# FNet plus MLP in one pass: a lighter warm-up, one block's layernorm and stores moved ahead of the prepared DFT weights, and one output moved ahead of a form

## The chip, the cores and the metric

The kernel runs on one core of a Trainium2 chip. Its time is the device time of one execution in microseconds (us). The core has TensorE (PE in the profile), VectorE (DVE), ScalarE (ACT), GpSimd (POOL) and SyncE (SP), each with an instruction stream of its own that runs in order; they wait for one another by semaphores. DMA transfers are issued from the queues of SP, ACT and POOL.

## What is computed

For x of 2048 tokens by 640 features, all in f32:

```python
xn = _layernorm(x, axis=-1)
a = einsum("bsd,ed->bse", xn, dft_hid_re)      # DFT over the 640 features
b = einsum("bsd,ed->bse", xn, dft_hid_im)
y = einsum("ts,bse->bte", dft_seq_re, a) - einsum("ts,bse->bte", dft_seq_im, b)
h = gelu(einsum("bsd,df->bsf", xn, w1) + b1)    # 640 -> 1536
return x + y + (einsum("bsf,fd->bsd", h, w2) + b2)
```

## The kernel before

Every product of two f32 matrices is made of three matmuls: each operand is split into a high part that is rounded to fp32r and a low part that is the rest, and high·high, high·low and low·high are added in PSUM. `split` is the helper for it: ScalarE copies the high part (L160 in the profile), VectorE subtracts for the low part (L161). A product of 128 by 128 by 512 is therefore three lines L278, L279, L280, or a row of L304 in the hidden layer.

**Blocks.** The tokens are four blocks of 512 (16 chunks of 128). The front loads chunks 0 to 3, centers them (ScalarE chunk 1, VectorE chunks 0, 2 and 3), transposes them on TensorE into five PSUM banks, and splits each bank into XT. Ten matmuls on zeros (`warm_up`) stand ahead of the transposes on TensorE. The scale of the layernorm of block 0 is multiplied in later, ahead of the gelu.

**The main loop** runs g over 24 units: 12 groups of 128 hidden features for block 0, then 12 for block 1. In iteration g, TensorE makes `hidden(g+2)` (15 matmuls) and `output(g)` (15 matmuls), ScalarE makes `gelu(g+2)` and its high part hs, VectorE the low part of hs. Beside that, `second_block(i)` in the second half (g = 12 + i) prepares blocks 2 and 3, whose hidden layers are computed later by a scheme of seven products instead of eight (`head`, `mid`, `finish`, with the sums of x called forms a11, a12, a22, oa, ob, s1 to s4, and sums of w1 called tw).

**What lies around the change.** For a block, the normalized x goes to DRAM (`ln_apply`, 16 transfers to xs, L203) and comes back in another layout (`load_z`, L234). `prep_w(s)` turns pieces of the two 640 by 640 DFT matrices (wraw, turned to wt), forms sums of them and splits them into the tile wst, from which POOL's queue stores them to DRAM (wit, L418). A place in wst is written again by later calls, so the write waits until the store from it has landed. When the early calls of `prep_w` are over, `open_tw` gives wst's memory to other tiles, the first of them tw0, which `split_w1(0)` writes. `load_xo(1)` loads x once more for block 1, and `outs_at` adds block 1's outputs to it: VectorE turns a PSUM bank (L371) and POOL adds it (L373). `forms_ob` subtracts on VectorE, splits tw1 and the form ob.

All orders are written out by hand: the order of calls in the code is the order on each engine, and no scheduler changes it. Pools only decide which memory a tile lies in, and so which earlier transfer a write waits for.

Of the kernel before, what the change touches and what calls it, by code (L numbers as in the profile page):

```python
# [15 lines left out]
P = 128  # L16
Q = 4
B = 32
EPS = 1e-5
NWARM = 10  # L20
TAIL = 4
ASIDE = 1
PADL = 8
# [3 lines left out]
def kernel(  # L27
# [126 lines left out]
    def split(hi, lo, src, perm=False):  # L154

        h, l, s = (hi, lo, src)
        if perm:
            h, l = chunked(hi), chunked(lo)
            s = src.rearrange("p (q c i) -> p q c i", q=Q, i=B)
        nc.scalar.activation(h, s, AF.Copy)  # L160
        nc.vector.tensor_tensor(l, s, h.bitcast(F32), op=ALU.subtract)  # L161
# [125 lines left out]
    def unit(g):  # L287
        return g if g < NF else LATE[g % NF]

    def hidden(g, aside=None):  # L290
# [4 lines left out]
        if g == 0:  # L295
            steps = FIRST
        if g == 1:

            steps.sort(key=lambda s: s[1] == 2)
        for n, (j, k) in enumerate(steps):  # L300
            if aside and n == ASIDE:
                aside()
            a, b = kinds[k]
            nc.tensor.matmul(  # L304
                acc, W1[i][:, a, j * P : (j + 1) * P], XT[j][:, b], start=n == 0, stop=n == len(steps) - 1
            )
        return acc


    FIRST = [(0, 0), (0, 2), (1, 0), (1, 2), (0, 1), (2, 0), (2, 2), (1, 1), (3, 0), (3, 2)]  # L310
    FIRST += [(2, 1), (4, 0), (4, 2), (3, 1), (4, 1)]

    def gelu(g, acc, fill=lambda k: None):

# [347 lines left out]
            slots[key] = t[:, k * 2 * D : (k + 1) * 2 * D].rearrange("p (a b) -> p a b", a=2)  # L662
    nc.gpsimd.memset(eps, EPS)
    make_identity(nc, ident)
    nc.vector.memset(zeros, 0.0)
    warm = whole["as"][:, :TB]
    nc.vector.tensor_copy(warm, zeros)

    nc.scalar.activation(eps[:, 1:2], eps[:, 0:1], AF.Sqrt)
    load_w1(0, cuts=(0, 2, ND))  # L670
    load_w1(1, cuts=(0, 2, ND))

    wacc = bank(0)

    def warm_up():
        nc.tensor.matmul(wacc, warm[:, :P], warm, start=True, stop=True)

    for k in range(NWARM):
        warm_up()
    load_w1(2)  # L680
    load_w2(0)
    nc.sync.dma_start(b1c, b1.rearrange("(i p) -> p i", p=P))
    load_w2(1)
# [7 lines left out]
    def transpose_x(c, j0, j1):  # L691
        for j in range(j0, j1):
            nc.tensor.transpose(tacc[j][:, c * P : (c + 1) * P], xp[:, c, j * P : (j + 1) * P], ident)
# [10 lines left out]
    def center(c, op, shift, j0=0, j1=ND):  # L704
        nc.vector.tensor_scalar(
            chunked(xp[:, c])[:, :, j0:j1],
            xt[c].rearrange("p (q c i) -> p q c i", q=Q, i=B)[:, :, j0:j1],
            shift,
            None,
            op0=op,  # L710
        )
# [7 lines left out]
    ln_stats(0)  # L719
    center(0, ALU.subtract, MV[:, 0, 0:1])  # L720
    ln_stats(2)
    center(2, ALU.subtract, MV[:, 2, 0:1])
    sum_on_act(3)
    center(3, ALU.add, MV[:, 3, 5:6], 0, 2)
    center(3, ALU.add, MV[:, 3, 5:6], 2, ND)
    for lo, hi in ((0, 2 * P), (2 * P, D)):
        h, l = (W1[0][:, k, lo:hi] for k in range(2))
        nc.scalar.activation(h, first_w1[:, lo:hi], AF.Copy)
        nc.vector.tensor_tensor(l, first_w1[:, lo:hi], h.bitcast(F32), op=ALU.subtract)
    transpose_x(0, 0, ND)  # L730
    transpose_x(1, 0, ND)
    warm_up()
    for j0, j1 in ((0, 2), (2, ND)):
        transpose_x(2, j0, j1)
        transpose_x(3, j0, j1)
    for j in range(ND):
        split(XT[j][:, 0], XT[j][:, 1], tacc[j])
    load_w1(3)
    load_w1(4)
    for q in range(Q):  # L740
        nc.sync.dma_start(b2c[q * B : (q + 1) * B], b2[q * DQ : (q + 1) * DQ].rearrange("(c i) -> i c", i=B))
    acc0 = hidden(0)
    prep_w1(1)
    acc1 = hidden(1)

    nc.gpsimd.tensor_scalar(MV[:, 1::2, 0], MV[:, 1::2, 5], -1.0, None, op0=ALU.mult)
    square_on_act(1)
# [236 lines left out]
    def second_block(i):  # L984

        if i == 0:
            load_z(2)
            ln_stats(12)
            ln_stats(13)
        if i == 1:  # L990
            ln_stats(14)
            ln_stats(15)
        if i == 2:
            ln_scale(12, 4)
            for c in range(12, 16):
                ln_apply(c, nc.gpsimd if c < 14 else nc.sync)
        if i == 3:
            A["zs"] = place("xc01", (P, 30 * P), F32, name="zs")
            turn_z2(two(0), 0)
            turn_z2(two(2), 2)  # L1000
            turn_z1(ZT[:, 0], 4)
            load_z(3)
        if i == 4:
            form_of("a11", 0, two(0)[:, 0], lane("as", 5))
            open_xf()
        if i == 5:
            form_of("a11", 1, two(0)[:, 1], lane("xc23", 0))
            form_of("oa", 0, ZT[:, 0], lane("xc23", 1))
        if i == 6:
            form_of("a12", 0, two(2)[:, 0], lane("xc23", 2))  # L1010
            turn_z2(ZT, 2)
            turn_z2(two(4), 0)
            turn_z1(A["zs"][:, 6 * TB : 7 * TB], 4)
            load_xo(1)
            open_tw()
        if i == 7:
            sums_w1(0)
            split_w1(0)
            load_rq(1)
            form_of("a22", 0, ZT[:, 0], lane("r01", 0))  # L1020
        if i == 8:
            form_of("a22", 1, ZT[:, 1], lane("r01", 1))
            add(ZT, ZT, two(4))
        if i == 9:
            form_of("s1", 0, ZT[:, 0], lane("r01", 2))
            form_of("s1", 1, ZT[:, 1], lane("r01", 3))
            add(two(4), two(0), two(4), ALU.subtract)
            add(ZT, ZT, two(0), ALU.subtract)
# [18 lines left out]
        form_of("s4", 0, two(2)[:, 0], XTT[:, 3])  # L1047
        form_of("s4", 1, two(2)[:, 1], XTT[:, 4])

    w_early = {0: (0,), 1: (1,), 2: (2,), 3: (3,), 4: (4,), 5: (5,)}  # L1050
    prep_w1(3)
    gelu(1, acc1)
    for g in range(NG):
        t, i = divmod(g, NF)
        if t == 0:
            if i:
                prep_w1(i + 3)
            prep_w2(i + 1)
            load_w1(i + 6)
            load_w2(i + 4)  # L1060
            if i != 8:
                first_block(i)
            if i == NF - 1:
                open_w()
                acc = hidden(g + 2)
                output(g)

                def fill(k):
                    for e in ((0,), (1, 2))[k]:
                        add_block(xo[0], e, oacc[0][e], f"ot0_{e}", bias=b2c[:, e : e + 1])  # L1070

                gelu(g + 2, acc, fill)
                outs(0, (3, 4))
            elif i == NF - 2:
                output(g)
                gelu(g + 2, hidden(g + 2))
            else:
                acc = hidden(g + 2) if g else acc2
                if i == NF - 3:
                    for j in range(ND):  # L1080
                        prep_xt(1, j)
                        if j + 2 < ND:
                            transpose_z(1, j + 2)
                gelu(g + 2, acc)
                if i == 8:
                    first_block(i)
                if i == 9:
                    ln_stats(10)
                    ln_stats(11)
                output(g)  # L1090
        elif i < NF - 2:
            acc = hidden(g + 2)
            gelu(g + 2, acc)
            output(g)
            second_block(i)
            for k in w_early.get(i, ()):
                prep_w(k)
# [708 lines left out]
```

## Time and profile before

| | us |
|---|---|
| median of 3 runs | 850.71 (850.18 to 850.97) |
| the profiled execution | 853.42 |
| its span | 851.6 |
| PE busy | 842.5 (99%) |
| DVE busy | 668.0 (78%) |
| ACT busy | 355.3 (42%) |
| POOL busy | 53.6 (6%) |
| granted TensorE clock | 0.999 |

The span runs from the first to the last instruction of the profiled execution; 853.42 is the time of that same execution from outside. Matmuls overlap in the profile: one is shown as 0.39 us long although the next starts 0.23 us later, so starts are compared, not durations. In brackets behind a row stands how long its engine had been idle and who ended that.

### The profile page before, as it was taken

How to read it: one execution, taken by the hardware profiler on the slowest of the kernel's cores; microseconds unless marked ns; L12 is line 12 of the kernel's file. 1: busy time of each engine (PE TensorE's matmuls, PEld its weight loads, DVE VectorE, ACT ScalarE, POOL GpSimd, SP SyncE). 2: the span in 40 equal slices, each digit the busy share in tenths (PEclk: the TensorE clock that was granted, in tenths of full speed). 3: DMA queues.
4: the chain of work that ended last, by engine and by line, in shares of the span. 5: the costliest groups of instructions: out<-in, count | busy, mean ns of one | idle time of the engine just before them, and what ended most of it. 6: DMA issues, size and time to landing. Idle time of an engine off the chain costs nothing.

```text
span 851.6 us, 10345 instructions
## 1 busy us (share of the span) xinstructions
PE 842.5 (99%) x3707; PEld 694.5 (82%) x3707; DVE 668.0 (78%) x841; ACT 355.3 (42%) x499; POOL 53.6 (6%) x78
## 2 busy tenths in 40 slices
PE   8999999999999999999999999999999999999997
PEld 6888888778888888888888888888888888888886
DVE  6766764795757888879988787899977898885687
ACT  7454533555655554333434343232322423223241
POOL 0000313131221300000000000000000000000001
PEclk9999999999999999999999999999999999999999
DMA  6667799738669998948743669763865879805464
GB/s 185 187 185 186 162 215 252 196 79 195 207 216 347 360 218 158 188 102 204 164 137 95 177 211 285 171 139 97 213 164 171 253 184 228 312 18 179 124 170 108
DMA packets 207363, 158.45 MB, mean 186 GB/s; under 512 B 81040, under 2 KB 180880, under 8 KB 206800
## 3 DMA queue, kind: packets, MB, share of 16 engines
q1 hardware_dynamic: 198368, 134.59, 62.2%
q0 software_dynamic: 4400, 21.89, 6.5%
q10 hardware_dynamic: 4544, 1.31, 0.6%
q8 instruction: 29, 0.48, 0.2%
q14 instruction: 22, 0.18, 0.1%
HBM read 114.76 MB, written 42.99 MB: 185 GB/s over the span
## 4 chain that ended last, share of the span: by engine, by line
PE 83%; DVE 4%; DMA 4%; ACT 3%; issue 3%; SPq 2%; POOL 1%; ACTq 0%; POOLq 0%; DVEq 0%
PE banks L278 27%; PE banks L279 26%; PE banks L280 26%; PE banks L304 3%; DMA x<-in_A_x_dram 1%; DMA wit<-wst 1%; SPq L388 1%; DMA xs<-x 1%; ACT ab L322 1%; SPq L203 0%; SPq L178 0%; POOL wit L418 0%; DVE r L161 0%; ACT hs L326 0%; DVE tw L161 0%
## 5 line engine op out<-in xcount | busy, mean ns | idle before, releaser
L278 PE MATMUL banks<-as,xab 128*128 128x512 f32 x411 | 160.0, 389 | 0.6 <-DVE zs L371 0.6
L279 PE MATMUL banks<-as,xab 128*128 128x512 f32 x411 | 159.9, 389 | 0.0
L280 PE MATMUL banks<-as,xab 128*128 128x512 f32 x411 | 159.9, 389 | 0.0
L160 ACT ACTIVATE as<-r 128x1024 fp32r<-128x1024 f32 x80 | 85.0, 1062 | 177.9 <-PE banks L280 149.5
L161 DVE TENSOR_TENSOR as<-r,as 128x1024 fp32r<-128x1024 f32 x80 | 97.1, 1215 | 41.5 <-ACT as L160 41.5
L278 PEld LDWEIGHTS banks<-as,xab 128*128 128x128 f32 x411 | 77.2, 188 | 17.0 <-DVE zs L371 1.0
L279 PEld LDWEIGHTS banks<-as,xab 128*128 128x128 f32 x411 | 77.2, 188 | 16.0
L280 PEld LDWEIGHTS banks<-as,xab 128*128 128x128 f32 x411 | 77.2, 188 | 15.9
L278 PE MATMUL banks<-as,xc 128*128 128x512 f32 x224 | 87.1, 389 | 0.0
L279 PE MATMUL banks<-as,xc 128*128 128x512 f32 x224 | 87.1, 389 | 0.0
L280 PE MATMUL banks<-as,xc 128*128 128x512 f32 x224 | 87.1, 389 | 0.0
L160 ACT ACTIVATE as<-rt 128x1024 fp32r<-128x1024 f32 x32 | 34.0, 1063 | 70.5 <-PE banks L280 62.5
L304 PE MATMUL banks<-xtt,xab 128*128 128x512 f32 x240 | 57.2, 391 | 0.2 <-ACT xtt L160 0.2
L304 PEld LDWEIGHTS banks<-xtt,xab 128*128 128x128 f32 x240 | 44.7, 188 | 10.1 <-ACT xtt L160 0.6
L278 PEld LDWEIGHTS banks<-as,xc 128*128 128x128 f32 x224 | 42.1, 188 | 8.8
L280 PEld LDWEIGHTS banks<-as,xc 128*128 128x128 f32 x224 | 42.1, 188 | 8.7
L279 PEld LDWEIGHTS banks<-as,xc 128*128 128x128 f32 x224 | 42.0, 188 | 8.7
L161 DVE TENSOR_TENSOR as<-rt,as 128x1024 fp32r<-128x1024 f32 x32 | 38.8, 1211 | 5.3 <-ACT as L160 5.3
L160 ACT ACTIVATE as<-u 128x1024 fp32r<-128x1024 f32 (+1 forms) x24 | 22.1, 919 | 48.2 <-PE banks L280 48.2
L512 DVE STREAM_TRANSPOSE r<-raw 128x1024 f32<-128x1024 f32 x32 | 39.5, 1239 | 3.0 <-PE banks L280 2.4
L161 DVE TENSOR_TENSOR as<-u,as 128x1024 fp32r<-128x1024 f32 (+1 forms) x24 | 24.9, 1041 | 18.8 <-ACT as L160 18.8
L512 DVE STREAM_TRANSPOSE rt<-raw 128x1024 f32<-128x1024 f32 x32 | 38.8, 1229 | 0.9 <-PE banks L280 0.8
(353 smaller groups left out, 1622.9 us busy)
## 6 DMA issues: line engine op xcount, KB each, us to landing
raw<-in_A_dft_seq_re_dram SPq DMA_DIRECT2D x64, 256.0 KB, 5.5
raw<-in_A_dft_seq_im_dram SPq DMA_DIRECT2D x64, 256.0 KB, 5.1
ws<-wit SPq DMA_DIRECT2D x15, 384.0 KB, 5.8
xo<-in_A_x_dram SPq DMA_DIRECT2D x16, 320.0 KB, 5.9
xab<-wit SPq DMA_DIRECT2D x13, 384.0 KB, 4.0
wit<-wstp POOLq DMA_DIRECT2D x12, 384.0 KB, 3.7
x<-in_A_x_dram SPq DMA_DIRECT2D x14, 320.0 KB, 4.4
xs<-x SPq DMA_DIRECT2D x56, 80.0 KB, 1.8
```

Source lines behind the costliest of these rows:

```text
L160: nc.scalar.activation(h, s, AF.Copy)
L161: nc.vector.tensor_tensor(l, s, h.bitcast(F32), op=ALU.subtract)
L278: nc.tensor.matmul(acc, wh, mh, start=first, stop=False, skip_group_check=goes_on)
L279: nc.tensor.matmul(acc, wh, ml, start=False, stop=False, skip_group_check=goes_on)
L280: nc.tensor.matmul(acc, wl, mh, start=False, stop=last, skip_group_check=goes_on)
L304: nc.tensor.matmul(acc, W1[i][:, a, j * P : (j + 1) * P], XT[j][:, b], start=n == 0, stop=n == len(steps) - 1)
L322: nc.scalar.activation(a, acc, AF.Gelu_apprx_tanh, bias=b1c[:, i : i + 1])
L388: nc.sync.dma_start(t[q * B : (q + 1) * B], v[:, :, s0 : s0 + B])
L512: nc.vector.transpose(held(pieces[g][2], u).rearrange("p c (n i) -> p c n i", i=B), r.rearrange("p n (c i) -> p c n i", i=B))
```

## The change

Three places change.

1. *Front.* The warm-up has 13 matmuls of 128 columns in f32 on a tile of zeros, instead of 10 (and one between the transposes) of 512 columns in fp32r on a copy of it. w1's second group is loaded in four transfers instead of eight, the third in eight instead of four. ScalarE centers the first 256 features of chunk 3; VectorE centers chunk 2 in two pieces. The second half of w1's first group is split after the first two XT instead of ahead of all. Three of the transposes come after the first two products, and hidden(0) and hidden(1) are issued by one function, `first_two`.
2. *Block 3.* Statistics, scale and stores of chunks 12 to 15 all come at i = 0, ahead of `load_z(2)` and of `prep_w(0)`. The calls of `prep_w` 3, 4 and 5 come one iteration later each (5 directly ahead of `open_tw`), and so do `split_w1(0)` and `load_rq(1)`; form a22 of half 0 comes ahead of them.
3. *Outputs of block 1.* Output 2 is added ahead of `forms_ob`, with output 1 left behind it.

```diff
-NWARM = 10
+NWARM = 13
 ...
+    def first_two():
+
+        kinds = ((0, 0), (0, 1), (1, 0))
+        second = sorted(((j, k) for j in range(ND) for k in range(3)), key=lambda s: s[1])
+        order = [(0, s) for s in FIRST[:13]] + [(1, s) for s in second[:2]]
+        order += [(0, FIRST[13]), (1, second[2]), (0, FIRST[14])] + [(1, s) for s in second[3:]]
+        for n, (g, (j, k)) in enumerate(order):
+            if n == 2:
+                transpose_x(3, 2, ND)
+                for e in range(2, ND):
+                    split(XT[e][:, 0], XT[e][:, 1], tacc[e])
+                prep_w1(1)
+            a, b = kinds[k]
+            ends = FIRST if g == 0 else second
+            nc.tensor.matmul(
...
-    nc.vector.memset(zeros, 0.0)
-    warm = whole["as"][:, :TB]
-    nc.vector.tensor_copy(warm, zeros)
+    nc.vector.memset(zeros[:, :P], 0.0)
 ...
-    load_w1(1, cuts=(0, 2, ND))
+    load_w1(1)
 ...
-        nc.tensor.matmul(wacc, warm[:, :P], warm, start=True, stop=True)
+        nc.tensor.matmul(wacc[:, :P], zeros[:, :P], zeros[:, :P], start=True, stop=True)
 ...
-    load_w1(2)
+    load_w1(2, cuts=(0, 2, ND))
 ...
-    center(3, ALU.add, MV[:, 3, 5:6], 0, 2)
-    center(3, ALU.add, MV[:, 3, 5:6], 2, ND)
-    for lo, hi in ((0, 2 * P), (2 * P, D)):
+    def split_first(lo, hi):
 ...
+    nc.scalar.activation(
+        chunked(xp[:, 3])[:, :, :2],
+        xt[3].rearrange("p (q c i) -> p q c i", q=Q, i=B)[:, :, :2],
 ...
+    center(2, ALU.subtract, MV[:, 2, 0:1], 0, 2)
+    center(2, ALU.subtract, MV[:, 2, 0:1], 2, ND)
+    split_first(0, 2 * P)
+    center(3, ALU.add, MV[:, 3, 5:6], 2, ND)
 ...
+    for j in range(2):
         split(XT[j][:, 0], XT[j][:, 1], tacc[j])
+    split_first(2 * P, D)
 ...
         if i == 0:
-            load_z(2)
-            ln_stats(12)
-            ln_stats(13)
-        if i == 1:
-            ln_stats(14)
-            ln_stats(15)
-        if i == 2:
+            for c in range(12, 16):
+                ln_stats(c)
             ln_scale(12, 4)
             for c in range(12, 16):
                 ln_apply(c, nc.gpsimd if c < 14 else nc.sync)
+            load_z(2)
 ...
             load_xo(1)
+            prep_w(5)
             open_tw()
         if i == 7:
             sums_w1(0)
+            form_of("a22", 0, ZT[:, 0], lane("r01", 0))
+        if i == 8:
             split_w1(0)
             load_rq(1)
-            form_of("a22", 0, ZT[:, 0], lane("r01", 0))
-        if i == 8:
 ...
-    w_early = {0: (0,), 1: (1,), 2: (2,), 3: (3,), 4: (4,), 5: (5,)}
+    w_early = {0: 0, 1: 1, 2: 2, 4: 3, 5: 4}
 ...
     outs(1, (0,), yt=lambda n: AB[:, 0], done=False)
+    outs_at((2,), (4,))
     forms_ob()
-    outs_at((2, 1), (4, 5))
+    outs_at((1,), (5,))
```

Lines below the front are 16 to 24 higher in the changed kernel. L278 to L280 stay, the matmul of `first_two` happens to be L304, `hidden` becomes L322, the gelu (L322 before) L340 and its hs (L326) L344.

On TensorE, the front of the program up to the first output products, before (xp is the centered x, xtt is XT, xab holds the split w1; L304 is the hidden layer, L336 and L337 the first outputs):

```order
L676 MATMUL banks<-as 128x512 x10
L693 MATMUL banks<-ident,xp 128x128 x10
L676 MATMUL banks<-as 128x512
L693 MATMUL banks<-ident,xp 128x128 x10
L304 MATMUL banks<-xtt,xab_122 128x512 x30
L304 MATMUL banks<-xtt,xab_123 128x512
L764 MATMUL banks<-ident,ab 128x128 x4
L304 MATMUL banks<-xtt,xab_123 128x512 x14
L336 MATMUL banks<-hs,rt_130 128x512
```

And on TensorE in the changed kernel, where L322 is the hidden layer from hidden(2) on:

```order
L692 MATMUL banks<-zeros 128x128 x13
L709 MATMUL banks<-ident,xp 128x128 x10
L692 MATMUL banks<-zeros 128x128
L709 MATMUL banks<-ident,xp 128x128 x7
L304 MATMUL banks<-xtt,xab_122 128x512 x2
L709 MATMUL banks<-ident,xp 128x128 x3
L304 MATMUL banks<-xtt,xab_122 128x512 x28
L322 MATMUL banks<-xtt,xab_123 128x512
L788 MATMUL banks<-ident,ab 128x128 x4
L322 MATMUL banks<-xtt,xab_123 128x512 x14
L354 MATMUL banks<-hs,rt_130 128x512
```

The warm matmuls are narrower, three transposes stand behind two products, and the rest of the row is the same.

On ScalarE, from prep_w(3) (its first four wst rows) over gelu(18) to gelu(19), before (wst is the staging tile, ab and hs belong to a gelu, as and xc to the forms of x):

```order
L160 ACTIVATE wst<-wt_1_1217 128x256
L160 ACTIVATE wst<-wt_1_1217 128x128
L160 ACTIVATE wst<-wt_1_1219 128x256
L160 ACTIVATE wst<-wt_1_1219 128x128
L322 ACTIVATE ab<-banks,b1c 128x512
L326 ACTIVATE hs<-ab 128x512
L160 ACTIVATE as<-zs 128x512
L160 ACTIVATE wst<-wt_1_1219 128x256
L416 ACTIVATE wst<-wt_1_1219 128x128
L160 ACTIVATE wst<-wt_1_1219 128x256
L160 ACTIVATE wst<-wt_1_1217 128x128
L322 ACTIVATE ab<-banks,b1c 128x512
```

And on ScalarE in the changed kernel, from gelu(18) (its hs is the row behind it) on:

```order
L340 ACTIVATE ab<-banks,b1c 128x512
L344 ACTIVATE hs<-ab 128x512
L160 ACTIVATE as<-zs 128x512
L160 ACTIVATE wst<-wt_1_1266 128x256
L160 ACTIVATE wst<-wt_1_1266 128x128
L160 ACTIVATE wst<-wt_1_1268 128x256
L160 ACTIVATE wst<-wt_1_1268 128x128
L340 ACTIVATE ab<-banks,b1c 128x512
L344 ACTIVATE hs<-ab 128x512
L160 ACTIVATE xc_127<-zs 128x512
L160 ACTIVATE xc_127<-zt 128x512
```

The gelu that stood behind the first four wst rows stands ahead of them, and the next one ahead of the second group.

On ScalarE around tw0, the first tile in wst's old memory (rq is the raw w1, r the place of form a22), before:

```order
L160 ACTIVATE wst<-wt_1_1217 128x256
L160 ACTIVATE wst<-wt_1_1219 128x256
L160 ACTIVATE wst<-wt_1_1217 128x256
L322 ACTIVATE ab<-banks,b1c 128x512
L326 ACTIVATE hs<-ab 128x512
L160 ACTIVATE xc_127<-zs 128x512
L322 ACTIVATE ab<-banks,b1c 128x512
L326 ACTIVATE hs<-ab 128x512
L160 ACTIVATE tw_1421<-rq_1273 128x1024
L160 ACTIVATE r_129<-zt 128x512
L322 ACTIVATE ab<-banks,b1c 128x512
```

And on ScalarE at the same place of the changed kernel:

```order
L340 ACTIVATE ab<-banks,b1c 128x512
L344 ACTIVATE hs<-ab 128x512
L160 ACTIVATE xc_127<-zs 128x512
L160 ACTIVATE wst<-wt_1_1266 128x256
L160 ACTIVATE wst<-wt_1_1268 128x256
L160 ACTIVATE wst<-wt_1_1266 128x256
L340 ACTIVATE ab<-banks,b1c 128x512
L344 ACTIVATE hs<-ab 128x512
L160 ACTIVATE r_129<-zt 128x512
L340 ACTIVATE ab<-banks,b1c 128x512
L344 ACTIVATE hs<-ab 128x512
L160 ACTIVATE tw_1459<-rq_1261 128x1024
```

A gelu is now ahead of the last three wst rows, and the first form into r and one more gelu are ahead of tw.

More of the change, by code (lines that the diff above doesn't have):

```diff
@@ L288, in unit @@
         return g if g < NF else LATE[g % NF]
+    def first_two():
[12 more added lines that the diff above has]
+            nc.tensor.matmul(
+                bank(g),
+                W1[g][:, a, j * P : (j + 1) * P],
+                XT[j][:, b],
+                start=(j, k) == ends[0],
+                stop=(j, k) == ends[-1],
+            )
+        return bank(0), bank(1)
     def hidden(g, aside=None):
@@ L294, in hidden @@
         steps = [(j, k) for j in range(ND) for k in range(3)]
[L295 to L299, printed above, removed]
         for n, (j, k) in enumerate(steps):
@@ L307, in hidden @@
         return acc
-    FIRST = [(0, 0), (0, 2), (1, 0), (1, 2), (0, 1), (2, 0), (2, 2), (1, 1), (3, 0), (3, 2)]
-    FIRST += [(2, 1), (4, 0), (4, 2), (3, 1), (4, 1)]
+    FIRST = [(0, 0), (0, 2), (1, 0), (1, 2), (0, 1), (2, 0), (1, 1), (3, 0), (2, 2), (3, 2)]
+    FIRST += [(4, 0), (4, 2), (2, 1), (3, 1), (4, 1)]
     def gelu(g, acc, fill=lambda k: None):
@@ L721 @@
     ln_stats(2)
-    center(2, ALU.subtract, MV[:, 2, 0:1])
     sum_on_act(3)
-    center(3, ALU.add, MV[:, 3, 5:6], 0, 2)
-    center(3, ALU.add, MV[:, 3, 5:6], 2, ND)
-    for lo, hi in ((0, 2 * P), (2 * P, D)):
+    def split_first(lo, hi):
         h, l = (W1[0][:, k, lo:hi] for k in range(2))
@@ L729 @@
         nc.vector.tensor_tensor(l, first_w1[:, lo:hi], h.bitcast(F32), op=ALU.subtract)
+    nc.scalar.activation(
+        chunked(xp[:, 3])[:, :, :2],
+        xt[3].rearrange("p (q c i) -> p q c i", q=Q, i=B)[:, :, :2],
+        AF.Identity,
+        bias=MV[:, 3, 5:6],
+    )
+    center(2, ALU.subtract, MV[:, 2, 0:1], 0, 2)
+    center(2, ALU.subtract, MV[:, 2, 0:1], 2, ND)
+    split_first(0, 2 * P)
+    center(3, ALU.add, MV[:, 3, 5:6], 2, ND)
     transpose_x(0, 0, ND)
@@ L732 @@
     warm_up()
[L733 to L736, printed above, removed]
+    transpose_x(2, 0, 1)
+    transpose_x(3, 0, 2)
+    transpose_x(2, 1, ND)
+    for j in range(2):
         split(XT[j][:, 0], XT[j][:, 1], tacc[j])
+    split_first(2 * P, D)
     load_w1(3)
@@ L741 @@
         nc.sync.dma_start(b2c[q * B : (q + 1) * B], b2[q * DQ : (q + 1) * DQ].rearrange("(c i) -> i c", i=B))
-    acc0 = hidden(0)
-    prep_w1(1)
-    acc1 = hidden(1)
+    acc0, acc1 = first_two()
     nc.gpsimd.tensor_scalar(MV[:, 1::2, 0], MV[:, 1::2, 5], -1.0, None, op0=ALU.mult)
@@ L1095 @@
             second_block(i)
-            for k in w_early.get(i, ()):
-                prep_w(k)
+            if i in w_early:
+                prep_w(w_early[i])
         elif i == NF - 2:
```

## The prediction

> **What bounds the kernel now.** I read the page's first lines, then the busy time by stretch.
>
> ```profile
> span 851.6 us, 10345 instructions
> PE 842.5 (99%) x3707; PEld 694.5 (82%) x3707; DVE 668.0 (78%) x841; ACT 355.3 (42%) x499; POOL 53.6 (6%) x78
> 100.00:185.00 85.00, 83.40 (x364) 67.85 (x363) 58.02 (x107) 37.24 (x71) 20.03 (x28) 1.00 0.74 188
> 185.00:845.00 660.00, 660.00 (x2911) 545.83 (x2910) 540.60 (x602) 260.93 (x337) 30.56 (x42) 1.00 0.69 188
> ```
>
> In the rows of stretches the second pair is PE's busy time. TensorE is full from 185 to 845 us and loses 1.6 us between 100 and 185. The change touches only the first 21 us and the work of about 106 to 188 us, so no more can be won than what PE loses there. The longest wait after the front, from the list of who makes PE wait:
>
> ```profile
> PE banks L278 <- DVE zs L371: 0.6, 1, 0.6
> ```
>
> That one belongs to the outputs of block 1 (zs is what they are turned into). PE's timeline shows the others (start, duration, what, and the idle time before with its releaser):
>
> ```profile
> 1.91 4.46 PE L676 MATMUL banks<-as 128*128 128x512 f32 x10 [1.91 <-DVE as L667]
> 9.66 7.54 PE L304 MATMUL banks<-xtt,xab 128*128 128x512 f32 x31 [0.20 <-ACT xtt L160]
> 20.70 0.39 PE L336 MATMUL banks<-hs,rt 128*128 128x512 f32 x1
> ...
> 143.10 0.39 PE L278 MATMUL banks<-hs,r 128*128 128x512 f32 x1
> ...
> 143.87 0.40 PE L280 MATMUL banks<-hs,r 128*128 128x512 f32 x1
> ...
> 146.87 3.56 PE L304 MATMUL banks<-xtt,as 128*128 128x512 f32 x15
> 150.83 0.49 PE L278 MATMUL banks<-hs,r 128*128 128x512 f32 x1 [0.39 <-ACT hs L326]
> 151.91 0.50 PE L279 MATMUL banks<-hs,r 128*128 128x512 f32 x1 [0.58 <-DVE hs L328]
> ...
> 155.21 3.56 PE L304 MATMUL banks<-xtt,xab 128*128 128x512 f32 x15
> 158.61 0.39 PE L278 MATMUL banks<-hs,r 128*128 128x512 f32 x1
> ```
>
> Undisturbed, fifteen products take 158.61 − 155.21 = 3.40 us, 0.2267 each. So the loss around 151 is 155.21 − 146.87 − 2 × 3.40 = **1.54 us**, and the one at 143 is 143.87 − 143.10 − 2 × 0.2267 = **0.32**. The cause stands on ScalarE:
>
> ```profile
> 146.71 0.42 ACT L160 ACTIVATE wst<-wt 128x256 fp32r<-128x256 f32 x1 [3.45 <-DMA wit<-wst]
> 148.92 0.62 ACT L160 ACTIVATE wst<-wt 128x256 fp32r<-128x256 f32 x2 [1.58 <-DMA wit<-wst]
> 149.44 0.67 ACT L322 ACTIVATE ab<-banks,b1c 128x512 f32<-128x512 f32 x1
> 154.70 1.26 ACT L160 ACTIVATE wst<-wt 128x256 fp32r<-128x256 f32 x3 [2.89 <-DMA wit<-wst]
> ```
>
> The gelu at 149.44 stands behind prep_w(4), whose writes to wst wait until earlier stores out of wst have landed. Last, the chain that ended last, between 150 and 187 us:
>
> ```profile
> 150.29 5.24 DMA wit<-wst
> ...
> 163.54 1.07 ACT tw L160
> ...
> 183.83 0.50 PE banks L278
> ...
> 186.85 0.47 PE banks L278
> ```
>
> It enters PE only at 183.83 and 186.85 (the first product of finish(0)). Before that it runs over a store, prep_w(5), the transposes of z, the sums of rq, tw0 and a long row of DVE work. This second chain is no more than a microsecond behind PE, and it decides how much of PE's gain is kept.
>
> **The change part by part.** *Front.* The first real product at 9.66 waits for XT and for a w1 split that came late:
>
> ```profile
> 8.59 0.52 ACT L728 ACTIVATE xab<-w1r 128x384 fp32r<-128x384 f32 x1 [0.85 <-DMA w1r<-in_B_w_dram]
> 12.48 0.74 ACT L160 ACTIVATE xab<-w1r 128x640 fp32r<-128x640 f32 x1 [0.93 <-DMA w1r<-in_B_w_dram]
> 7.44 1.20 DVE L705 TENSOR_SCALAR xp<-x,mv 128x640 f32<-128x640 f32 x3
> ```
>
> Now the second half of w1(0), which waited 0.85 us for its load, is split after XT 0 and 1, and three transposes less stand ahead. ScalarE takes a 256-wide piece of chunk three's centering off DVE's 1.20 us (three pieces; some 0.33). The first product can then start at about 8.9, but product three waits for its XT and splits 2 to 4 come 0.52 later behind the moved half: the gain by the first output product (20.70) is between 0 and 9.66 − 8.9 = 0.76. The other limits on that product also move: w1(1)'s last load is the 12th on SP's queue instead of the 16th, so the 0.93 us wait at 12.48 shrinks, while w1(2) has eight loads instead of four, the total unchanged. I take **−0.55**.
>
> The warm products are 13 of 128 columns instead of 10 of 512, in plain f32, starting about 0.7 earlier, without the cast. The trace has no such product. Nearest above is a 512-wide one, 4.46 / 10 = 0.446: 13 make 5.8 us, ending near 7.0, after the 6.39 of today, yet the last transposes wait for centering until 8.11, so it costs nothing:
>
> ```profile
> 6.39 1.28 PE L693 MATMUL banks<-ident,xp 128*128 128x128 f32 x10
> 8.11 1.35 PE L693 MATMUL banks<-ident,xp 128*128 128x128 f32 x10 [0.21 <-DVE xp L705]
> ```
>
> Nearest below is such a transpose, 1.28 / 10 = 0.128: 13 make 1.7 us, ending near 3, and PE then idles for three microseconds. Today's warm products cost 0.446 against 0.2267 later, so a stretch of slow products precedes the fast ones; were it only postponed, products after 9 us would cost 0.22 more each, for up to as many as ran slow today (ten): at most +2.2. The trace cannot choose between the two. I put nothing into the sum, because PE's spare time near 184, worked out below, covers the lower row as well; the lower row stays as a rival. The Trainium skill (FP8 and Floating Point Precision, TensorE Precision Notes) says true f32 takes four passes through the array; by it a 128-wide f32 product would cost as much as a 512-wide one in a single pass, which is the upper row, and the front keeps its gain. No run here shows it yet.
>
> *Order of block 3 and prep_w.* On ScalarE gelu(18) goes ahead of prep_w(3), gelu(19) ahead of prep_w(4), gelu(20) ahead of prep_w(5), and block 3's square root (with its table loads) lies at i = 0. That removes the 0.32 and the 1.54, **−1.86**, as far as PE goes. No instruction is added. What moves: the 16 stores of xs (80 KB each) now stand ahead of the first wit stores on POOL and ahead of z2 and wraw(1) on SP. Today's places on those queues:
>
> ```profile
> 134.28 5.92 SPq L203 DMA_DIRECT2D xs<-x  x8
> 155.87 1.60 POOL L418 DMA_DIRECT2D wit<-wst  x3 [5.04 <-DVE wst L161]
> ```
>
> Eight SP stores issue in 5.92 us, so z2's load, which went ahead of them, and with it block 2's transposes and prep_w(3), come 2 to 6 us later. The cover is that PE needs none of it before head(0), and that DVE has room (58.02 busy of 85 us). I cost it at nothing here; if prep_w runs late it shows in tw0, next. One gelu does stand behind a prep_w still: gelu(19) behind prep_w(3), which needs wraw(1) and the stores of prep_w(2). Should those land late, PE waits there as it does at 150.83 today, up to the 1.54 again; I leave that to the range.
>
> *tw0.* It lies in wst's memory, so it waits for prep_w(5)'s three stores. Today those are issued from 155.87 on, before xo(1)'s load, and the transposes of z3 follow:
>
> ```profile
> 158.45 1.24 DVE L786 STREAM_TRANSPOSE zt<-z 128x1024 f32<-128x1024 f32 x1
> 161.33 0.65 DVE L328 TENSOR_TENSOR hs<-ab,hs 128x512 fp32r<-128x512 f32 x1
> ...
> xo<-in_A_x_dram SPq DMA_DIRECT2D x4, 320.0 KB, 5.4
> wit<-wst POOLq DMA_DIRECT2D x3, 256.0 KB, 2.6
> ```
>
> In the changed order prep_w(5) stands behind those transposes, 161.33 − 158.45 = 2.9 us, and xo(1)'s load is issued ahead of it. With gelu(20) freed and PE some 2.4 ahead the transposes start near 156 and end near 159; the three wst pieces (1.26 us in the row of 154.70) and their stores follow until about 160.5, beside 4 × 320 KB of xo. The last two rows give the time from issue to landing, 2.6 us for a store alone, 5.4 for xo: the last store lands between 162 and 166, and I take the early end, 163, since the first two stores go out while xo's first pieces are still being issued. tw0, at 163.54 today, comes at **about 163.0** (161.5 if the transposes start earlier still, 166 with all of it slow).
>
> From tw0 to finish(0) the trace has 186.85 − 163.54 = 23.3 us. The first a22 form and one gelu's low half now go before tw0:
>
> ```profile
> 165.77 0.69 DVE L161 TENSOR_TENSOR r<-zt,r 128x512 fp32r<-128x512 f32 x1
> ...
> 167.00 0.68 DVE L161 TENSOR_TENSOR r<-zt,r 128x512 fp32r<-128x512 f32 x1
> ```
>
> 167.00 − 165.77 = **−1.2**. Against it stands outs(2) ahead of forms_ob():
>
> ```profile
> 164.63 1.23 DVE L161 TENSOR_TENSOR tw<-rq,tw 128x1024 fp32r<-128x1024 f32 x1 [1.13 <-ACT tw L160]
> 180.24 2.31 DVE L161 TENSOR_TENSOR tw<-rq,tw 128x1024 fp32r<-128x1024 f32 x1
> 179.35 2.12 POOL L373 TENSOR_TENSOR xo<-xo,ab 128x512 f32<-128x512 f32 x1 [21.88 <-DVE ab L371]
> 183.86 5.50 POOL L373 TENSOR_TENSOR xo<-xo,zs 128x512 f32<-128x512 f32 x4 [2.39 <-DVE zs L371]
> ```
>
> The same tw split took 2.31 instead of 1.23 while POOL added an output: the two take turns, at about 1.1 us per POOL addition. With outs(2) first, two POOL additions fall on the subtraction and the tw1 split: **+0.9** (0 to +1.4, the step of the four at 183.86 being 5.50 / 4 = 1.38). The Trainium skill (SBUF — State Buffer, Who interferes with whom) says that a DVE instruction with two SBUF inputs contends for a shared port with a GpSimd instruction that reads SBUF, the loser blocking fully. The rows agree, 2.31 against 1.23; the rule speaks against this edit. In return PE's 0.6 wait at 183.83 (head(1)) falls, since the bank it needs is freed by outs(2).
>
> Sum on the second chain: tw0 163.0 + 23.3 − 1.2 + 0.9 gives finish(0) at 186.0 instead of 186.85: **−0.85**. Sum on PE: 186.85 − 0.55 − 1.86 − 0.6 = 183.8. The later one decides, so most of PE's gain of 3.0 turns into waiting near 184. After 190 us the rows stay the same. So the kernel gains 0.8 us. The profiled execution was 853.42 us with 1.8 outside its span, 2.7 above the median of the runs, 850.71; I take the difference from the median: **849.9 us**.
>
> **The rivals.** *All of it is kept (0.27).* If prep_w(5)'s stores land by 161.5, tw0 starts two microseconds earlier and finish(0) stands at 184.5, near PE's own 183.8: −2.3, **848.4**; −3.0 (847.7) at the most. For it: a store alone needs 2.6 us. Against: xo(1) is issued first.
>
> *The second chain gets longer (0.13), slower.* Xs stores and z2 ahead of wraw(1) delay prep_w(3) to prep_w(5); the stores of prep_w(4), 5.24 us in the chain, run in the traffic of block 3's z. If tw0 starts after 163.8 the change loses: 186.85 − 23.3 + 1.2 − 0.9 = 163.85 is that point. At 166 it is +2.1, **852.8**. For it: both ScalarE's waits (3.45 and 2.89) and the chain hang on these stores. Against: DVE is idle for a third of 100 to 185 and can catch up.
>
> *The light products do not warm the array (0.05).* Then +2.2 in front, of which PE's spare time near 184 (186.0 − 183.8 = 2.2) hides all: −0.8 to 0, about **850.4**.
>
> *Nothing comes of it (0.05).* Every gain ends in waiting at 184: **850.7**.
>
> **How the numbers follow.** My forecast, −1.7 to +0.3, has 0.50. A measurement of this kernel can tell about 0.2%, 1.7 us, from no change. Faster by more: the kept gain and a little of the forecast's edge, 0.28. Slower by more: most of the longer chain, 0.10. Within: 0.62. The range reaches from 848.2 (−2.5, most of the kept gain) to 852.0 (+1.3, a tw0 at 165.1).
>
> **What would show it.** Right: no PE wait between 140 and 160, the first output product near 20.1, tw0 at 162 to 164 behind wit stores, and a PE wait of a microsecond or two shortly before finish(0), put down to DVE. Wrong: a tw0 before 161.5 (more gain) or after 163.9 (loss), a new PE wait in 125 to 150 on a form or on XT, warm products far from 0.44 us each, or a different sum after 190 us.

## The result, and the profile after

The changed kernel takes 857.88 us (median of 6 runs, 856.72 to 859.46) against 850.48 (6 runs, 850.12 to 850.97): 7.4 us slower, ratio 1.0087, 95% interval 1.0074 to 1.010. The forecast was 0.8 us faster, with 852.0 as the end of the range.

The first lines of its page, its stretches (the second pair of numbers is PE's busy time) and what PE waited for:

```profile
span 856.4 us, 10378 instructions
PE 844.2 (99%) x3724; PEld 696.7 (81%) x3724; DVE 666.3 (78%) x840; ACT 356.3 (42%) x500; POOL 54.0 (6%) x78
100.00:185.00 85.00, 81.99 (x357) 66.40 (x355) 54.74 (x105) 37.29 (x72) 20.33 (x29) 1.00 0.73 188
185.00:845.00 660.00, 657.71 (x2899) 544.25 (x2899) 540.47 (x600) 263.30 (x342) 32.72 (x42) 1.00 0.69 187
PE banks L278 <- DVE zs L389: 2.1, 1, 2.1
PE banks L278 <- ACT banks L881: 1.8, 2, 1.5
PE banks L692 <- DVE zeros L683: 1.0, 1, 1.0
PE banks L278 <- ACT r L160: 1.0, 1, 1.0
PE banks L322 <- ACT xab L160: 0.4, 1, 0.4
PE banks L279 <- DVE r L161: 0.2, 1, 0.2
```

The waits at 150 us are gone, as forecast. New ones stand between 173 and 190 us: on a form in r, on a copy of a bank by ScalarE (L881) and on zs in `head(1)`. They lie ahead of `finish(0)`, and the chain below leads from tw0 to it. (The 0.4 on xab is a late split of w1 at 31 us. It costs more than the row says: the hidden layers around it start at 23.52, 31.13 and 38.51, where 6.80 lie between two of them elsewhere, so 1.4 us are lost. front_only and after_two_fixes, below, load w1 in the same way and do not have it; whether most executions of the changed kernel have it is not known.) PE has 17 matmuls more than before (3724 for 3707); that will matter.

The chain of waits of the changed kernel, near the place where it joins PE, and the rows of SP, POOL and ScalarE around it:

```profile
163.05 5.86 DMA wit<-wst
169.13 1.07 ACT tw L160
...
191.97 0.50 PE banks L278
```

```profile
116.06 4.29 POOL L203 DMA_DIRECT2D xs<-x  x8 [8.70 <-DVE x L201]
146.00 1.15 POOL L436 DMA_DIRECT2D wit<-wst  x2 [10.42 <-DVE wst L161]
161.99 1.60 POOL L436 DMA_DIRECT2D wit<-wst  x3 [5.10 <-DVE wst L161]
...
119.05 8.63 SPq L203 DMA_DIRECT2D xs<-x  x8
127.73 2.84 SPq L234 DMA_DIRECT2D z<-xs  x4
130.67 8.44 SPq L406 DMA_DIRECT2D wraw<-in_A_dft_hid_re_dram  x4
142.56 1.90 SPq L234 DMA_DIRECT2D z<-xs  x4
161.42 2.61 SPq L381 DMA_DIRECT2D xo<-in_A_x_dram  x4
...
153.53 0.42 ACT L160 ACTIVATE wst<-wt 128x256 fp32r<-128x256 f32 x1 [5.40 <-DMA wit<-wst]
169.13 1.06 ACT L160 ACTIVATE tw<-rq 128x1024 fp32r<-128x1024 f32 x1 [6.78 <-DMA xo<-in_A_x_dram]
```

The 16 stores of xs go first; z2's load is issued at 127.73 and wraw(1)'s at 130.67; prep_w(3)'s stores are issued at 146.00, behind the load of block 3's z (142.56), and hold up prep_w(4) until 153.53; prep_w(5)'s stores are issued from 161.99 on, among the pieces of xo(1), and the last lands 5.86 us after its issue. tw0 starts at 169.13. (The last row names xo because xo was the nearer transfer; the chain names the store, which tw0's memory waits for.) From tw0 to `finish(0)` there are 191.97 − 169.13 = 22.8 us.

### The profile page after: what moved, and what is told of

Same layout as the page of the kernel before. It is cut to its first block, busy times and chain, and to the rows that moved or that the text cites. A ratio compares the mean times of both kernels' runs of the same rounds, so it can differ in the third digit from the quotient of the medians.

```text
span 856.4 us, 10378 instructions
## 1 busy us (share of the span) xinstructions
PE 844.2 (99%) x3724; PEld 696.7 (81%) x3724; DVE 666.3 (78%) x840; ACT 356.3 (42%) x500; POOL 54.0 (6%) x78
## 4 chain that ended last, share of the span: by engine, by line
PE 80%; DMA 5%; issue 5%; DVE 5%; ACT 2%; SPq 2%; POOL 1%; ACTq 0%; POOLq 0%; DVEq 0%
PE banks L278 26%; PE banks L279 26%; PE banks L280 26%; PE banks L322 2%; DMA x<-in_A_x_dram 1%; DMA xs<-x 1%; DMA z<-xs 1%; POOL wit L436 1%; DMA wit<-wst 1%; SPq L256 1%; DMA w2r<-in_B_w_dram 1%; DVE st L185 1%; SPq L203 1%; DVE xtt L161 0%; DVE zt L238 0%
## 5 line engine op out<-in xcount | busy, mean ns | idle before, releaser
L280 PE MATMUL banks<-as,xab 128*128 128x512 f32 x411 | 160.1, 390 | 0.0
L278 PE MATMUL banks<-as,xab 128*128 128x512 f32 x411 | 160.1, 390 | 0.0
L280 PEld LDWEIGHTS banks<-as,xab 128*128 128x128 f32 x411 | 77.2, 188 | 16.0
L278 PEld LDWEIGHTS banks<-as,xab 128*128 128x128 f32 x411 | 77.2, 188 | 16.0
L280 PE MATMUL banks<-as,xc 128*128 128x512 f32 x224 | 87.3, 390 | 0.0
L278 PE MATMUL banks<-as,xc 128*128 128x512 f32 x224 | 87.3, 390 | 0.0
L322 PE MATMUL banks<-xtt,xab 128*128 128x512 f32 x210 | 50.6, 392 | 0.6 <-ACT xab L160 0.4
L280 PEld LDWEIGHTS banks<-as,xc 128*128 128x128 f32 x224 | 42.1, 188 | 8.7
L278 PEld LDWEIGHTS banks<-as,xc 128*128 128x128 f32 x224 | 42.1, 188 | 8.7
L322 PEld LDWEIGHTS banks<-xtt,xab 128*128 128x128 f32 x210 | 39.1, 188 | 9.6 <-ACT xab L160 0.9
```

The source lines that it names most:

```text
L278: nc.tensor.matmul(acc, wh, mh, start=first, stop=False, skip_group_check=goes_on)
L280: nc.tensor.matmul(acc, wl, mh, start=False, stop=last, skip_group_check=goes_on)
L322: nc.tensor.matmul(acc, W1[i][:, a, j * P : (j + 1) * P], XT[j][:, b], start=n == 0, stop=n == len(steps) - 1)
```

## The experiments

The kernel before was run again beside the others; its medians beside the rows of the table were 850.47 (the first three), 850.75 (the next four), 850.64 (the next three) and 850.71 (the last three). The ratios are not those of the medians: prep_only's median is 1.15 us above the one beside it, its ratio 1.0006 with an interval that reaches 1.0018.

| kernel | median us | ratio to before (95%) |
|---|---|---|
| front_only | 852.86 | 1.0029 (1.0017 to 1.0041) |
| mid_only | 856.47 | 1.0068 (1.0055 to 1.0081) |
| outs_only | 851.07 | 1.0006 (0.9997 to 1.0015) |
| stats_only | 856.78 | 1.0069 (1.0055 to 1.0082) |
| prep_only | 851.90 | 1.0006 (0.9995 to 1.0018) |
| mid_xo_late | 852.87 | 1.0022 (1.0012 to 1.0032) |
| front_z3_late | 852.26 | 1.0014 (1.0005 to 1.0024) |
| front_warm512 | 850.30 | 0.9993 (0.9984 to 1.0002) |
| warm_only | 853.00 | 1.0028 (1.0018 to 1.0039) |
| stats_z2_first | 856.86 | 1.0076 (1.0063 to 1.0088) |
| front_warm5 | 851.96 | 1.0013 (1.0004 to 1.0022) |
| after_two_fixes | 852.87 | 1.0023 (1.0013 to 1.0032) |
| best_try | 850.12 | 0.9988 (0.9980 to 0.9997) |

### Was the profile of before like its other executions?

> The kernel before, unedited, once more, with a new profile. The recorded profile of before took 853.42 us, 2.7 over the median of its runs; it shows PE losing 1.5 us around 151 and 0.6 at 183.8. If those losses belong to every execution (theory A), a new profile shows them again at the same places and takes about 853. If they were the slow part of one execution's DMA landings (theory B), a profile at about 850.5 has less of them: PE loses about 1 us in all between 100 and 190 instead of 3, and the change had that much less to win.

It took 850.06 us. PE's whole list of waits, its stretch from 100 to 185, and the rows that stand for the chain to tw0:

```profile
PE banks L676 <- DVE as L667: 1.9, 1, 1.9
100.00:185.00 85.00, 85.00 (x376) 70.22 (x375) 60.98 (x111) 38.77 (x73) 23.03 (x31) 1.00 0.76 191
120.40 1.98 SPq L234 DMA_DIRECT2D z<-xs  x4
138.62 1.15 POOL L418 DMA_DIRECT2D wit<-wst  x2 [6.11 <-DVE wst L161]
139.68 2.22 SPq L234 DMA_DIRECT2D z<-xs  x4
143.85 0.67 ACT L322 ACTIVATE ab<-banks,b1c 128x512 f32<-128x512 f32 x1
159.97 1.06 ACT L160 ACTIVATE tw<-rq 128x1024 fp32r<-128x1024 f32 x1 [4.56 <-DVE rq L452]
183.63 0.49 PE L278 MATMUL banks<-r,tw 128*128 128x512 f32 x1
```

PE waits for nothing after the front. Here prep_w(3)'s stores (138.62) are issued ahead of block 3's z (139.68); gelu(19) runs at 143.85 where the first profile had it at 149.44, and tw0 at 159.97 for 163.54. In the first profile the second of those stores was issued behind the first quarters of z and took to 148.84 (this landing is from its trace's DMA records). The waits of 1.54 and 0.6 us that the change was to remove belong to a slower execution, not to the kernel as it mostly runs. The last row is the first product of `finish(0)`: 183.63 here, 186.85 in the first profile and 191.97 in the changed kernel, 8.3 us later than here. The two profiled times, 858.18 and 850.06, differ by 8.1.

### The three parts, each alone

```diff
 # kernel before, with one part of the change each
 # front_only: part 1    mid_only: part 2    outs_only: part 3
```

> The front's edits alone on the kernel before. In the profile of the changed kernel the first output product came 0.58 us earlier (20.12 for 20.70), but PE then lost about 1.1 us at 30 to 32 us, behind the split of the fourth group of w1, which landed at 23.05 instead of 21.34. Stores theory: the front is worth between -0.6 and +0.5 us, within the noise: 850 to 851. Rival, that the front carries the loss: +2 us or more, above 852.5.

> Block 3's statistics, scale and stores ahead, prep_w(3) to (5), split_w1(0), load_rq(1) and form a22 later; the front and the outputs as before. Stores theory: the whole loss is here, since z2 and wraw(1) land 4 us later, prep_w(3)'s stores run beside the load of z3, prep_w(5)'s beside xo(1), and tw0 starts near 169 instead of 163.5: +5 to +7 us, 856 to 858. Rival, that the outputs' order (POOL and DVE taking turns) or the front carries it: under +2, below 852.5.

> Only output 2 of block 1 added ahead of forms_ob. Stores theory: two POOL additions meet the subtraction and the split of tw1, +0.8 to +0.9 on the way to finish(0), of which 0 to 0.9 reaches the end: 850.5 to 851.4. Rival, that this order carries the loss: +2 or more.

Two of the three are slower: +2.4 us in front, where I had expected noise and the rival +2 or more, and +6.0 in the second part. The outputs' order is within what can be told. Its tw1 split took 2.31 us, but so it does in the kernel before, where one POOL addition already falls on it; what grew is the subtraction ahead of it, 1.99 us for 1.18. The parts' sum is 9.0 for 7.4 measured, so they overlap by 1.6.

### The second part: which of its edits

```diff
 # stats_only: before, with only the order at i = 0
-load_z(2); ln_stats(12); ln_stats(13)     (14, 15 at i = 1; scale and stores at i = 2)
+ln_stats(12..15); ln_scale(12, 4); ln_apply(12..15); load_z(2)
 # prep_only: before, with prep_w(3..5), split_w1(0), load_rq(1) later, form a22 ahead
 # stats_z2_first: stats_only, with load_z(2) put first again
```

> Of the second part only the order at i = 0: statistics, scale and stores of chunks 12 to 15, then load_z(2); prep_w, tw0 and xo(1) as before. Theory 1 (the stores and z2 ahead of wraw(1) make prep_w(3) late, and its stores then run beside the load of z3): wraw(1) lands near 144 for 136.9, tw0 starts 4 to 6 us after the 159.97 of the undisturbed profile, and most of the 6 us of mid_only is here: 854 to 856. Theory 2 (prep_w(5) behind the turned z3 and beside xo(1) is what costs): the order at i = 0 alone stays under 852.

> Of the second part only the rest: prep_w(3), (4), (5) an iteration later, split_w1(0) and load_rq(1) later, form a22 ahead; block 3's statistics and z2 as before. Theory 1: wraw(1) lands as before (about 137), prep_w(3)'s stores miss less of z3's traffic, prep_w(5)'s stores still meet xo(1): +1 to +3, 851.5 to 853.5. Theory 2: nearly all of the loss, 855 to 857.

> stats_only (the order at i = 0, which carried 6 us), but with z2's load put first again, so that only the statistics and the 16 stores stand ahead of prep_w(0) and wraw(1). If the cost is that z2 and with it wraw(1) start late (issued at 127 and 130 instead of 120 and 123), most of it comes back, 851 to 853. If the 16 stores ahead of the wit stores and of wraw(1) are enough by themselves, 855 to 857 stays.

The order at i = 0 alone costs as much as the whole second part, the rest alone little or nothing, and putting z2 first brings nothing back. That z2's place might be the cost was wrong; in stats_z2_first SP's rows read

```profile
114.55 3.40 SPq L930 DMA_DIRECT2D ys<-xo  x1
124.82 2.03 SPq L234 DMA_DIRECT2D z<-xs  x4
127.26 7.94 SPq L203 DMA_DIRECT2D xs<-x  x8
135.30 2.42 SPq L388 DMA_DIRECT2D wraw<-in_A_dft_hid_re_dram  x4
```

z2 lies in xo(0)'s memory and waits for the last ys store, which now lands behind POOL's eight xs stores (z2 at 124.82; 120.40 in the repeated profile of before), and wraw(1) follows SP's eight. The 16 stores, with the statistics ahead of them, are enough by themselves. In stats_only the gelus behind prep_w(3) and prep_w(4) pay all of the price, as PE's timeline shows:

```profile
140.05 3.56 PE L304 MATMUL banks<-xtt,as 128*128 128x512 f32 x15
145.82 0.50 PE L278 MATMUL banks<-hs,r 128*128 128x512 f32 x1 [2.21 <-ACT hs L326]
...
149.72 0.63 PE L278 MATMUL banks<-hs,r 128*128 128x512 f32 x1
150.15 0.55 PE L279 MATMUL banks<-hs,r 128*128 128x512 f32 x1
...
151.47 3.56 PE L304 MATMUL banks<-xtt,as 128*128 128x512 f32 x15
```

The two hidden layers start 11.42 us apart for 6.80, so 4.6 are lost: 2.21 of waiting, and then products that start 0.43 apart instead of 0.23 until 150.15, with a granted clock of 0.64 between 145.8 and 150.2 (1.00 ahead and behind). The next hidden layer starts at 159.69, another 1.4 lost. tw0 comes at 165.34, and PE waits for nothing behind it. In mid_only and the changed kernel the gelus are ahead, PE does not wait at 150, and the late stores are paid through tw0 instead. That stats_only and mid_only both lose 6.0 us is chance: they lose them at different waits.

### Whether xo(1) makes prep_w(5)'s stores late

```diff
-            load_xo(1)
             prep_w(5)
...
             load_rq(1)
+            load_xo(1)
```

> mid_only, but xo(1)'s load stands behind rq(1)'s on SP's queue, and so behind tw0: prep_w(5)'s three stores have the DMA engines to themselves. In mid_only's like, the changed kernel, they were issued at 162.0 to 163.1 and landed at 167.1 to 168.9 with xo, tw0 at 169.13. If xo's traffic costs that (both theories), the stores land 2.6 us after issue, tw0 starts near 165.7, 3 us earlier, and 3 us come back: 853 to 854. If tw0 waits for something else, nothing comes back: 856.5. A risk: xo lands near 176, close to its first use at 179 to 183.

POOL's stores and tw0, first in mid_only, then in mid_xo_late:

```profile
159.74 1.60 POOL L418 DMA_DIRECT2D wit<-wst  x3 [5.10 <-DVE wst L161]
168.04 1.06 ACT L160 ACTIVATE tw<-rq 128x1024 fp32r<-128x1024 f32 x1 [7.94 <-DMA xo<-in_A_x_dram]
```

```profile
159.64 1.60 POOL L418 DMA_DIRECT2D wit<-wst  x3 [5.09 <-DVE wst L161]
163.59 1.06 ACT L160 ACTIVATE tw<-rq 128x1024 fp32r<-128x1024 f32 x1 [3.58 <-DMA wit<-wst]
```

The stores are issued at the same time, and tw0 starts 4.4 us earlier without xo beside them; 1.0068 becomes 1.0022. This is the place where the second part's delay turns into time. (prep_only has its stores beside xo(1) too, and tw0 at 164.0, but without the 16 stores ahead they are issued four microseconds earlier, at 155.79.)

### What the front costs

```diff
 # front_z3_late: front_only, and
-            load_z(3)                  (i = 3, SP's queue)
+            load_z(3, nc.scalar)       (i = 4, ScalarE's queue, behind gelu(18))
```

> front_only, but block 3's z is loaded from ScalarE's queue behind gelu(18), after prep_w(3)'s splits, instead of ahead of them on SP's queue. front_only lost 2.4 us, and its profile shows the waits at 150 and 183.8 that the first profile of before has and its repetition has not: wraw(1) landed at 139.4 instead of 136.9 and prep_w(3)'s stores came behind z3 (landed 146.1 and 148.4 for 141.2 and 143.3). If that race between the stores and z3 is what front_only lost, the waits go and the time is 849.5 to 850.8. If the front loses it elsewhere, 852.5 to 853.5 stays.

A part seems to come back (1.0014 for 1.0029, with intervals that overlap) and the waits at 150 go, but tw0 still comes at 161.94. So the race with z3 is only where the delay shows; it begins earlier. Traces of all kernels point to the load of block 1's z, whose first transpose on VectorE waits for it. Before (repeated) and front_only, with the load's issue:

```profile
69.92 1.91 SPq L234 DMA_DIRECT2D z<-xs  x4
78.33 0.71 DVE L238 STREAM_TRANSPOSE zt<-z 128x512 f32<-128x512 f32 x1 [0.45 <-DMA z<-xs]
```

```profile
69.92 1.91 SPq L234 DMA_DIRECT2D z<-xs  x4
79.58 0.71 DVE L238 STREAM_TRANSPOSE zt<-z 128x512 f32<-128x512 f32 x1 [1.70 <-DMA z<-xs]
```

Same issue, 1.25 us later. The DMA queues show one difference there. For the window from 76 to 79 us, front_only has the first row and the repeated before has none of that queue; from 79 to 82 the repeated before has the second row and front_only none:

```profile
q8 instruction: 1, 0.02, 2.8%
q8 instruction: 1, 0.02, 2.1%
```

It is one packet of 16 KB of kind "instruction", a fetch of program code. In front_only it falls into z's last quarter, in before into the load of x behind it, which nobody waits for yet. All sixteen profiles agree: in the four kernels with 3724 matmuls the fetch starts between 77.0 and 78.2 us, and z's last quarter lands 8.0 to 8.4 us after its issue; in the twelve with 3707 or 3708 it starts between 79.7 and 81.0, and the quarter takes 6.7 to 7.1. Why it moves: PE's count.

```profile
1.04 5.39 PE L692 MATMUL banks<-zeros 128*128 128x128 f32 x26 [1.04 <-DVE zeros L683]
```

Thirteen f32 products are 26 matmul records (and 26 weight loads), so 14 light products are 28 matmuls for the 11 of before.

```diff
 # front_warm512: front_only with the old warm-up (10 and 1 products, 512 columns, fp32r)
 # warm_only:     before with the new warm-up alone
 # front_warm5:   front_only with NWARM = 5 (10 and 2 matmuls)
```

> front_only, but with the old warm-up: ten and one products of 512 columns in fp32r on a cast copy of zeros. In the traces an f32 product of 128 columns is two PE instructions (13 show as 26), so the light warm-up adds 17 matmul instructions to PE's stream; every fetch of PE's code (16 KB, the queue called instruction) comes about 3 us earlier for it, and the one at 80 us (before) stands at 77 us, where it runs beside the load of block 1's z: that load took 8.1 us from the issue of its last quarter instead of 6.9, and everything fed by it (xo(0), the stores, x 12 to 15, both wraw, prep_w, tw0) is over a microsecond later. Fetch theory: with the old count the fetch is back at 80, z lands after 6.9, the waits at 150 and 184 go, 849.6 to 850.4. Rival, that the front's other edits (order of loads, splits, transposes) cost it: 852.5 to 853 stays.

> The kernel before with the light warm-up alone (13 and one f32 products of 128 columns). Fetch theory: 17 more PE instructions, the fetch at 77 us, z of block 1 lands over 1 us later, waits at 150 and 184 as in front_only: 852 to 853.5, against 850.5. Rival: nothing, 850 to 851, since the warm-up ends before the transposes are waited for.

> front_only with five light warm-up products ahead of the transposes instead of 13: with the one between the transposes six f32 products, 12 matmul instructions, against 11 in the kernel before and 28 in front_only. Fetch theory (the count of PE instructions places the fetch of PE's code at 77 or 80 us): the fetch is back near 80, block 1's z lands 6.9 us after its last issue, 849.7 to 850.8, with a few tenths lost in front if the first products run slow. Rival (something else about light f32 products costs, such as the clock or the early start): 852.5 to 853.5 stays.

| kernel | PE matmuls | fetch in window | z's first issue to first transpose, us |
|---|---|---|---|
| before, repeated | 3707 | 79 to 82 | 78.33 − 69.92 = 8.41 |
| front_warm512 | 3707 | 79 to 82 | 78.19 − 69.68 = 8.51 |
| front_warm5 | 3708 | 79 to 82 | 79.43 − 70.94 = 8.49 |
| front_only | 3724 | 76 to 79 | 79.58 − 69.92 = 9.66 |
| warm_only | 3724 | 76 to 79 | 80.50 − 70.74 = 9.76 |
| changed kernel | 3724 | 76 to 79 | 80.88 − 70.97 = 9.91 |

The warm-up alone makes the kernel 2.4 us slower, and taking it alone out of the front gives 2.6 back. (The profile of front_warm512 is of its slowest run, 852.07, with tw0 at 162.2: fetch and z are in place there, so something else can make tw0 late as well.) front_warm5 was expected at 849.7 to 850.8 and took 851.96: the fetch and z are back in place and PE waits for nothing in the middle, but five light products are too short a warm-up:

```profile
1.04 2.50 PE L692 MATMUL banks<-zeros 128*128 128x128 f32 x10 [1.04 <-DVE zeros L683]
6.33 2.37 PE L709 MATMUL banks<-ident,xp 128*128 128x128 f32 x10 [2.78 <-DVE xp L721]
...
21.47 0.39 PE L354 MATMUL banks<-hs,rt 128*128 128x512 f32 x1
```

PE idles 2.78 us, the ten transposes take 2.37 us instead of 1.28 in the changed kernel, and the first output product comes at 21.47 instead of 20.44 in front_only and in the repeated before: 1.0 us, most of its distance of 1.25 from before. So the light products as such do not cost the 2.4 us; their count does. That the same count added at another place would do the same was not tried.

### Do the two causes add up, and what is left of the change

```diff
 # after_two_fixes: the changed kernel, with the old warm-up and xo(1) behind rq(1)
 # best_try: after_two_fixes, with the order at i = 0 to 2 and the outputs as before
```

> The changed kernel with two edits: the old warm-up (front_warm512 gave 2.4 us back against front_only) and xo(1) loaded behind rq(1) (mid_xo_late gave 3.6 back against mid_only). If the two causes add, 857.9 - 2.4 - 3.6 = 851.9, 851.3 to 852.7. If they overlap in the chain to tw0, 853 to 855.

> What the runs leave standing: the front with the old warm-up, prep_w(3) to (5) and tw0 later with xo(1) behind rq(1); block 3's statistics, z2 and the outputs' order as before. If the waits in some executions of before come from prep_w(5) and xo(1), this has fewer of them: 849.5 to 850.2. If only the front counts, as front_warm512: 850.3.

The two fixes give 5.0 of the changed kernel's 7.4 us back, 852.87, with 851.45 to 854.62 over 12 runs: 1.0 less than their sum, between the two expectations. What stays, 2.2 us with tw0 at 162.38, goes when best_try puts the order at i = 0 and the outputs back; the outputs alone were 0.6. best_try has the lowest median, 0.12% under before (interval 0.03 to 0.20%, which overlaps that of front_warm512), and its 11 runs stay within 849.58 to 850.50. The 29 runs of before beside it reach from 850.05 to 853.38. In its trace tw0 starts at 157.62, 2.3 us ahead of the repeated before, which leaves that much more room for a late landing.

## Why the prediction was wrong

Three steps failed: what there was to win, the 16 stores and the lighter warm-up that were put down at nothing, and the early end that was taken for the last stores ahead of tw0.

**What bounds.** Losses of 1.54, 0.32 and 0.6 us were read from one execution that was 2.7 us above the median, and the difference was then taken off the median. The repeated profile has none of them. The numbers at hand said so: 853.42 stood above all runs shown.

**Front, −0.55.** As a duration it held: the first output product starts at 20.44 to 21.15 in the nine profiles with the old order of the front (mean 20.80), and at 20.07 to 20.44 in the six with the new one and a full warm-up (mean 20.22). The warm product cost 5.39 / 13 = 0.415 us, near the upper row. The Trainium skill (FP8 and Floating Point Precision, TensorE Precision Notes) gives true f32 four passes; this price agrees with it. What I missed is that it is two instructions. The lighter warm-up, put down at nothing, cost 2.4 us, 60 us downstream.

**"The 16 stores ... I cost it at nothing".** This is the largest mis-sized term: 6.0 us alone (stats_only), and 4.9 as the step from prep_only to mid_only. I had the delay nearly right, 2 to 6 us (z2's load came 6.1 later than in the profile that I read), and its cover wrong. The cover was said to be that PE needs none of it before head(0); it was used up by the wait for wst and by the gelu or tw0 behind that.

**tw0, 163.0 with 166 as its far end.** It came at 169.13. Block 3's transposes did not start near 156: they stood behind prep_w(4), which waited 5.40 us for prep_w(3)'s stores, and ran at 158.43 as before. The stores went out from 161.99 on, where the working had them done being issued by 160.5, and the last took 5.86 us beside xo(1), where I had taken the early end.

**From tw0 to finish(0), 23.3 − 1.2 + 0.9 = 23.0.** Measured 22.8, and the outputs' order cost 0.8 on it (1.96 for 1.18 in the subtraction beside POOL), near the +0.9. The break-even of 163.85 held only against the profile that it was worked out from: 169.13 − 163.85 = 5.3, and the spans, 856.4 and 851.6, differ by 4.8. For the kernel as it mostly runs, with `finish(0)` at 183.63, the same sum gives 183.63 − 23.0 = 160.6. So the forecast's own tw0 at 163.0 was already a loss of 2.4 us, outside the range. This later break-even fits the others: after_two_fixes has tw0 1.8 behind it, and its span is 1.6 longer than the repeated before's.

**The rivals.** The one that came was "the second chain gets longer", given 0.13 and priced at +2.1. Its mechanism and its place were right, its price less than half. That the light products cost 2.4 us, and the rival of the cold array said +2.2, is chance: that rival had the loss in the front, and the front's products come no later.

## What to carry to other kernels

Before you cost a stall away, see that it is in more than one execution: a profile that took longer than the plain runs shows stalls that most of them may not have. A transfer moved ahead must be followed to every queue and buffer behind it until a wait ends, above all where a staging tile is reused and a store must land first; the three stores of prep_w(5) landed 2.3 to 2.7 us after their issue alone (mid_xo_late) and 5.1 to 7.0 beside xo(1) (the changed kernel and mid_only). And count instructions, not only time: here 17 cheap matmuls more moved a fetch of program code onto a load that mattered.

## What was not expected of the hardware

A fetch of 16 KB of program code lasts 1.0 to 1.3 us near 80 us; moved 3 us by 17 matmuls, it made a load of four times 320 KB land 1.25 us later, and the kernel 2.4 us slower. That it delays the load by sharing one of the 16 DMA engines with it is inferred from its being one packet. That it is PE's code is inferred too: its place follows PE's count, and the 29 fetches of the repeated before are 28.8 us apart on average, the time of 127 products at 0.2267. An f32 product of 128 columns is two matmul records, of 0.207 us each in the changed kernel's first microseconds. After 2.2 us of waiting in stats_only the granted clock fell to 0.64 for some four microseconds, so that wait cost about twice its length. What made the first profile of before slow is not settled: its fetch at 80 stood as in the repeated profile (80.3 for 80.0), the next one came at 109.2 for 107.8, its loads of wraw and stores of ys landed one to three microseconds later from 110 us on, and no edit was found that brings this about.
